# A memory-attention and gated feed-forward block: a shorter feature map, statistics on ScalarE, reciprocal rows through DRAM, later gates and a new sorting of the plan

## The chip, the cores and the metric

The kernel runs on one core of a Trainium2 chip. The core has a matrix engine (TensorE, PE in the profile, with its weight loads as PEld), a vector engine (VectorE, DVE), an engine for functions (ScalarE, ACT), a general engine (GpSimd, POOL) and a queue that issues all of this kernel's DMAs (SyncE, SP). Each engine works through its own list of instructions in a fixed order and waits on semaphores. The metric is the device time of one execution in microseconds, and the median of three runs is compared.

## What is computed

The input x has 2048 tokens of width 1024 in bfloat16. The first block is attention with a compressive memory, 32 heads of width 32 (`Dh`), over four segments of 512 tokens:

```python
x = A_x
h = x + _A_ref(_layernorm(x), wq, wk, wv, wo, beta)
h2 = h + _B_ref(_layernorm(h), w1, w3, w2)      # silu(x@w1) * (x@w3) @ w2, width 3584
...
phi = lambda t: jnp.where(t > 0, t + 1.0, jnp.exp(t))
g = _sigmoid(beta)
for s in range(4):                               # M and z start at zero
    p = _softmax(qs @ ks.T * Dh ** -0.5 + mask)  # causal, within the segment
    a_mem = (phi(qs) @ M) / (phi(qs) @ z + 1e-06)
    o = g * a_mem + (1.0 - g) * (p @ vs)
    M = M + phi(ks).T @ vs
    z = z + phi(ks).sum(0)
```

The normalisation has no weights. Only x, the weights and `beta` are read; the other input of the second block is not used.

## The kernel before

**Stages.** `run` (L1402) registers the operations: constants and the normalisation, transposition and first projections of segment 0 (`constants`, `first_half`), normalisation of the other three segments (`ln1`), then for each segment the projections of the next one (`qkv`) and two halves of attention with 16 heads each (`attention`). The output projection with the residual and the second normalisation of four token tiles of 128 (`wo_stage`) follows for segment 0 after its attention, for segment 1 inside segment 2, for segments 2 and 3 inside the feed-forward part. That part has two blocks of 1024 tokens: `ffn_up` in 14 chunks of 256 columns and `ffn_down`.

**One half of attention.** Heads are packed in groups of four, one head (`j`) to each 32 partitions. `scores` computes key-by-query scores in ten steps (`i` 0 to 9). Each step fills PSUM banks 0 to 3 (L1094), ScalarE takes the exponential of 2048 columns into tile `et[i]` (L1108), and POOL zeroes the upper triangle by `affine_select` (L1117). Steps 0 to 4 belong to the first pair of groups, steps 5 to 9 to the second. `gather` (L1122) adds the exponentials of several key chunks into `sums` on DVE (L1128), so that the denominators need fewer columns. `finish` (L1145) then issues the numerators (one matmul block for each `j`, 16 matmuls, L1180), the denominators against a tile of ones (48 matmuls, L1180, into bank 4, preceded in segments 1 to 3 by four matmuls for the memory's denominator, L1173) and the memory update phi(k) times v (L1022, into bank 7). `DEN_AT = 2` registers the denominators after the numerators of `j` 0 and 1; the planner is free to turn that round.

**Reciprocals.** The denominators are transposed on DVE (`T1`, L1211), 1e-6 is added to the memory's part, and the reciprocal is taken (`Rc`, L1222). Row 0 of `Rc` belongs to the softmax, row 1 to the memory. The softmax part is spread over the partitions by two DVE transposes of a broadcast (`spread` into `R0`, L1243), and four products `Nsb * R0` follow on POOL or DVE (L1274). The memory part in segment 1 is spread in the same way into `R1`. In segments 2 and 3 (`ROWS`), `copies` does it through DRAM: a POOL copy, a DVE transpose into `T2`, a DMA to `r_scr` and four DMAs that each read four rows for all of 32 partitions (L1263). `retrieve` is held back until step `LATE` (3) of the next half; it multiplies phi(q) with the memory (L1292), combines the result with `gcol` and `R1` on DVE (L1305), which frees PSUM banks 0 to 3, and adds it into `oT` (L1308).

**Feature map.** `phi` (L985) works on 1024 columns at a time, 12 times for keys and 12 times for queries. The exponential is taken on ScalarE into the single buffer `phe` (L712 in the profile), DVE limits it to 1 (L989), the positive part of the input is taken on POOL, ScalarE or DVE as the planner decides (L993, L994), and DVE adds the two (L998). For keys the result is transposed by a DMA (`pkn`); for queries it goes to `pq`, which the retrieve of the half before still reads.

**Normalisation.** `ln` (L867) takes the statistics by `ln_stats` on DVE (two `bn_stats`, one `bn_aggr`, L861 and L864), or by `ln_act` on ScalarE with two passes that accumulate, if the tile's number is in `ON_ACT`. Tiles 0 to 15 are those of x and 16 to 31 those of h. In the kernel before `ON_ACT` is empty; only `first_tile` uses `ln_act`, for tiles 1 and 3. The reciprocal square root is on POOL.

**Gates.** `constants` (L798) loads `beta`, takes tanh(beta/2) on ScalarE in four operations and makes `gcol` (the gate) and `ocol` (one minus the gate) on DVE (L826, L828). They are first needed by the copies of the numerators into `Nsb` (L1231, L1232).

**Order of the work.** The order on each engine is not that of registration. `Graph` collects operations with their dependences, and `schedule` simulates the five engines in advance: at each moment a free engine takes, among operations whose inputs would be there, the one with the lowest class (`cls`), and among those the lowest sequence number. The durations in this simulation are written into the kernel: `dve_ns`, `act_ns`, `pool_ns` and `mm_ns`, and for a DMA 1.9 us after its bytes at 260 bytes a nanosecond, all DMAs one after another. The resulting order is emitted as it is. Where an operation takes longer on the chip than in the plan, the engines behind it wait. Groups of operations that share a PSUM bank take it when it is free: the dense matmuls of projections and of the feed-forward part use banks 5, 6 and 7 (after the attention the others too), and have the lower priority, so that they fill the time between the steps of attention. `port=True` in an operation tells the planner that DVE and POOL hold each other up. `SHIFT` gives for each unit of work (`stage()` starts one) an offset of the sequence number and of the class.

Of the kernel before, what the change touches and what calls it, by code (L numbers as in the profile page):

```python
# [18 lines left out]
DEN_AT = 2  # L19
DIRECT = False  # L20
BOTH2 = True
ROWS = (2, 3)
ADDED = ((1, 2, 3),) * 4
ON_ACT = ()
# [3 lines left out]
    3: (-320, -1), 4: (0, 1), 5: (-481, 0), 6: (-334, -1), 7: (365, 0), 8: (-1541, -1),  # L28
    9: (99, -1), 10: (865, 1), 11: (368, -1), 13: (140, 0), 14: (6, -1), 15: (18, 0),
    16: (-1206, 0), 17: (-918, 0), 18: (-6, 1), 19: (-488, 0), 20: (-215, 1), 21: (414, 1),  # L30
    23: (-58, 0), 24: (0, 1), 25: (-7, 0), 26: (-82, -1), 28: (-682, -1), 29: (-1308, -1),
    30: (-6603, 0), 31: (429, -1), 32: (-651, 0), 33: (-3176, 0), 34: (-496, 0), 35: (-1076, 0),
    36: (-624, 0), 37: (-1589, 0), 38: (0, -1), 39: (-4, 0), 40: (-277, 0), 41: (-320, 1),
    42: (-3785, 1), 43: (-148, 0), 44: (1693, 0), 45: (72, 0), 46: (275, 0), 48: (1583, 1),
    49: (299, 0), 50: (1122, -1), 51: (-1111, 0), 52: (-3085, 0), 53: (1277, 0), 54: (1912, 1),
    55: (491, 0), 56: (52, 0), 57: (-78, 0), 58: (-1228, 0), 59: (-7, 0), 60: (-103, 0),
    61: (501, 0), 62: (-112, 1), 63: (89, 0), 64: (-177, -1), 65: (-1143, 0), 66: (228, -1),
    67: (3315, -1), 68: (484, 0), 69: (-163, 1), 70: (2537, 1), 71: (-380, 0), 72: (833, 0),
    73: (1731, 0), 75: (-2092, -1), 76: (-155, 0), 77: (839, 1), 79: (108, 0), 80: (0, 1),
    81: (338, 1), 82: (697, 1), 83: (-320, 0), 84: (285, 0), 85: (1217, -1), 86: (-2242, 0),  # L40
    87: (-180, -1), 88: (2991, 1), 90: (1277, 0), 91: (252, -1), 92: (1203, 1), 93: (2098, 0),
    94: (5, 0), 95: (1349, 0), 98: (-244, -1), 99: (-14, 0), 100: (1667, 1), 101: (-47, 0),
    102: (-85, 1), 103: (1174, 0), 106: (-1638, 1), 107: (1004, 1), 108: (-1222, 1),
    109: (-48, -1), 110: (2537, 0), 111: (-15, 1), 112: (-447, 0), 113: (1690, 1),
    114: (-550, 0), 115: (-277, 0), 116: (-328, 1), 117: (1477, -1), 118: (37, 0),
    119: (-36, 0), 120: (-1378, -1), 121: (-1111, 1), 122: (232, -1), 123: (-401, 0),
    124: (-488, 1), 125: (94, 1), 127: (66, -1), 128: (252, 0), 129: (255, -1), 130: (501, -1),
    132: (28, 0), 134: (2, 1), 135: (856, -1), 136: (95, 0), 137: (482, 0), 139: (158, 1),
    140: (-291, 0), 142: (447, 0), 143: (-390, -1), 144: (90, -1), 145: (1198, 1),
    146: (200, 0), 147: (-180, 0), 148: (-885, -1), 149: (0, 1), 150: (-1249, 0), 151: (256, 0),  # L50
    152: (-567, -1), 153: (1731, 1), 154: (206, 0), 155: (-1573, 1), 156: (278, 0),
    158: (2418, 0), 159: (-1065, 1), 160: (1955, 1), 161: (288, -1), 162: (1035, 0),
    163: (-1029, 0), 164: (-1294, 1), 166: (60, -1), 167: (-1, 0), 168: (-846, 0),
    169: (255, 0), 171: (959, 1), 172: (-62, 1), 173: (-714, 0), 174: (-77, 0), 175: (716, -1),
    176: (-158, 0), 177: (117, 0), 178: (-3360, 1), 179: (153, -1), 180: (-594, 0),
    181: (-875, 0), 182: (-1181, 1), 184: (14, 1), 185: (-1260, 1), 186: (-2791, 1),
    187: (-183, -1), 188: (0, 1), 189: (1102, -1), 191: (-526, 0), 192: (-372, 0), 193: (0, -1),
    194: (25, 1), 195: (466, 0), 196: (-1098, 1), 197: (182, 1), 198: (-410, 1), 199: (0, 1),
    200: (-350, 1), 201: (-704, 1), 202: (17, 0), 203: (-224, 0), 204: (-1609, -1),
    206: (491, 0), 207: (37, 1), 208: (-945, 0), 209: (-2625, -1), 210: (1203, 0),  # L60
    211: (-734, 1), 213: (1780, 1), 214: (618, 1), 215: (-271, 0), 219: (-57, 0), 220: (0, -1),
    221: (547, -1), 222: (1095, 1), 223: (-4674, -1), 224: (-159, 0), 225: (69, 0),
    226: (62, 0), 227: (-44, -1), 229: (1014, 1), 230: (-818, 0), 231: (610, 1), 232: (92, 1),
    233: (1, -1), 234: (-337, 1), 235: (724, 0), 237: (269, 0), 238: (-488, 0), 240: (694, 1),
    241: (1020, 0), 243: (-219, 1), 244: (-349, 1), 245: (-238, -1), 246: (-1310, -1),
    247: (1154, -1), 248: (351, -1), 250: (581, 0), 251: (-68, 0), 252: (-940, 1),
    253: (365, 0), 254: (466, -1), 255: (-4, 0), 256: (-1012, 0), 257: (1144, 0), 258: (432, 0),
    259: (88, 0), 260: (3, 1), 261: (80, 0), 262: (-4, 0), 263: (64, 1), 265: (223, -1),
    266: (-216, -1), 267: (-860, 0), 268: (-236, -1), 269: (1156, 0), 270: (-238, 1),
    271: (-107, 1), 272: (432, 1), 273: (-432, 0), 274: (-3355, 1), 275: (1256, 1),  # L70
    276: (1764, 1), 277: (-77, 0), 278: (-279, 0), 279: (-567, 0), 280: (-2286, 1),
    281: (-89, 0), 282: (-3, 0), 283: (-69, -1), 284: (-111, -1), 285: (-2, 0), 286: (-110, 1),
    287: (-370, 0), 288: (-52, 0), 289: (-1782, -1), 290: (-1781, -1), 291: (45, 0),
    293: (-846, -1), 294: (521, 0), 295: (-1210, 0), 296: (1213, 1), 297: (696, 1),
    298: (967, 0), 299: (-16, 0), 300: (-138, 0), 301: (20, 0), 302: (1085, 0), 303: (9, 0),
    304: (-1097, 1), 305: (-649, 1), 306: (-2220, 1), 307: (0, -1), 308: (-635, 0),
    309: (10, 0), 310: (596, 1), 311: (694, 0), 312: (316, 1), 314: (1928, 1), 315: (-123, 0),
    316: (-138, -1), 317: (166, 0), 318: (612, 0), 319: (416, -1), 320: (1725, -1),
    321: (857, 0), 322: (278, -1), 323: (1764, 0), 324: (-69, 0), 326: (366, 1), 327: (-79, 0),
    328: (-1240, 0), 329: (356, 0), 330: (1509, 0), 331: (-1173, 0), 332: (284, -1),  # L80
    334: (715, 0), 335: (1178, -1), 336: (0, -1), 337: (82, -1), 338: (-85, 0), 339: (-308, 0),
    340: (-186, -1), 341: (-228, 0), 342: (-1134, 1), 344: (-424, 0), 345: (221, 0),
    346: (269, 0), 347: (1885, -1), 348: (1209, 0), 349: (690, 0), 350: (50, 0), 351: (-777, 0),
    352: (2, 0), 353: (-1040, 0), 354: (-6, 0), 355: (96, 1), 356: (952, 0), 357: (274, 0),
    358: (-6, -1), 359: (142, -1), 360: (-51, 1), 361: (-4, 0), 362: (25, 0), 363: (85, 0),
    364: (313, -1), 365: (-53, -1), 366: (693, -1), 367: (-158, 1), 368: (-612, -1),
    369: (173, 0), 370: (-1556, -1), 373: (-163, 1), 375: (-1005, 0), 376: (220, 0),
    377: (-15, 0), 379: (173, -1), 380: (13, 0), 381: (577, 0), 382: (1277, 0), 384: (0, -1),
    386: (2981, 0), 387: (953, 1), 388: (3969, 0), 389: (-280, 0), 390: (-238, 0),
    391: (281, 0), 392: (27, -1), 393: (-1832, 1), 394: (1902, 1), 395: (-131, 0),  # L90
    396: (1049, 0), 399: (-17, -1), 400: (381, 0), 401: (-259, -1), 402: (597, 0),
    403: (-240, -1), 404: (-1784, -1), 405: (5, 1), 406: (-7, 0), 407: (906, 0), 408: (274, 0),
    409: (-1006, 0), 410: (-8, -1), 411: (58, 0), 412: (-27, 0), 414: (1052, -1),
    415: (-766, 0), 418: (-9, 0), 419: (-1, -1), 420: (2, 0), 421: (-7, 0), 423: (-22, 0),
    428: (-8, 0), 431: (-3, 0), 432: (40, 0), 433: (235, 0), 435: (-1134, 0), 436: (92, 0),
    437: (-751, -1), 438: (1339, -1), 439: (4, -1), 441: (977, -1), 443: (-1217, 0),
    444: (-3, 0), 446: (1178, -1), 447: (-687, -1), 448: (467, 0), 449: (-246, 0),
    450: (-18, 0), 451: (3, 0), 452: (1, 0), 453: (-4, 0), 454: (-120, 0), 457: (26, 0),
    459: (110, 0), 460: (-976, -1), 461: (99, 0), 462: (792, 0), 465: (1926, 0), 466: (347, 0),
    467: (3, 1), 468: (1, 1), 469: (-860, 1), 470: (2868, 0), 471: (267, 0), 473: (-7, 0),  # L100
    475: (-523, -1), 476: (-1557, -1), 477: (-1805, 0), 478: (-79, 0), 479: (-689, 0),
    480: (0, -1), 481: (9, 1), 482: (-6, -1), 483: (-149, 1), 484: (-481, 0), 485: (34, 0),
    486: (-27, 0), 487: (-1251, 0), 488: (-6, 0), 489: (0, -1), 490: (-1298, 1), 494: (445, 0),
    495: (185, -1), 496: (631, -1), 497: (-933, 0), 498: (45, 0), 499: (326, 0), 500: (4, 0),
# [483 lines left out]
def dve_ns(n, mode=1):  # L588
    return 150.0 + n / (0.96 * mode)
# [897 lines left out]
```

## Time and profile before

| | |
|---|---|
| timed runs | 894.58 us median of 3 (892.8 to 895.2) |
| profiled execution | 890.75 us, span 889.0 us, granted clock 1.0 |
| TensorE busy | 881.4 us (99%) |
| VectorE busy | 465.9 us (52%) |
| ScalarE busy | 298.9 us (34%) |
| GpSimd busy | 205.7 us (23%) |

TensorE counts as busy from the start of a matmul to its modelled end, and matmuls overlap, so small waits between two of them are seen better from the starts in the timeline than from the busy share. The first 420 us hold all of the attention, and there DVE is at 14 to 20 of each 22 us, ScalarE at 12 to 17 in most and POOL at 5 to 16. From 420 us on TensorE works through feed-forward matmuls only, together with the output projections of segments 2 and 3. The chain of work that ended last, in order of time, tells at each point which engine TensorE waited for.

### The profile page before, as it was taken

Reading aid. Unit: us, or ns where it says so; the run is one execution under the profiler, and the core shown is the slowest. Engines: PE = TensorE matmul, PEld = TensorE weight load, DVE = VectorE, ACT = ScalarE, POOL = GpSimd, SP = SyncE. Lnnn points to the kernel's source line nnn. Section 1 sums busy time; section 2 is a strip of 40 time slices with the busy share of each in tenths; the row PEclk is TensorE's granted clock in tenths of the full one; section 3 lists DMA queues with packets and bytes.
Section 4 is the critical chain, followed back from the end, with each engine's and each line's share of the span. In section 5 each row is a group of like instructions: output and inputs, shape, how many; then the busy total and the mean of one; then the engine's idle time right before and its main releaser. Section 6 shows DMA issues by size and latency. Waiting matters only on the chain.

```text
span 889.0 us, 13629 instructions
## 1 busy us (share of the span) xinstructions
PE 881.4 (99%) x5821; PEld 398.2 (45%) x5821; DVE 465.9 (52%) x710; ACT 298.9 (34%) x319; POOL 205.7 (23%) x239
## 2 busy tenths in 40 slices
PE   8999999999999999999999999999999999999998
PEld 5344444443444344444444444444444444444445
DVE  5796988779786879774546311212234343332111
ACT  5767776767555656521111100000112111110000
POOL 3747364656462735310100000000000000000000
DMA  7889958563652418195437310013131321301111
GB/s 237 235 170 227 236 154 172 184 144 107 170 139 71 132 58 180 51 305 143 170 90 178 100 43 24 30 48 95 48 95 48 112 72 49 94 1 29 42 36 48
DMA packets 148027, 101.55 MB, mean 114 GB/s; under 512 B 46080, under 2 KB 134144, under 8 KB 147456
## 3 DMA queue, kind: packets, MB, share of 16 engines
q1 hardware_dynamic: 147968, 100.69, 42.9%
q8 instruction: 46, 0.75, 0.4%
q14 instruction: 13, 0.11, 0.0%
HBM read 80.75 MB, written 9.44 MB: 101 GB/s over the span
## 4 chain that ended last, share of the span: by engine, by line
PE 92%; POOL 3%; DMA 2%; DVE 2%; SPq 1%; issue 0%; ACT 0%
PE ps L737 86%; PE ps L1180 3%; PE ps L1094 3%; SPq L314 1%; POOL pq L994 1%; DMA beta<-in_A_beta_dram 1%; DMA R<-r_scr 1%; POOL oT L1308 0%; POOL Nsb L1274 0%; DVE pq L998 0%; POOL et L1117 0%; DMA r_scr<-T 0%; PE ps L1022 0%; POOL pk L994 0%; DVE R L1305 0%; PE ps L1292 0%
## 5 line engine op out<-in xcount | busy, mean ns | idle before, releaser
L737 PE MATMUL ps<-hnT,w1b 128*128 128x512 bf16 x896 | 220.2, 380 | 0.0
L737 PE MATMUL ps<-hnT,w3b 128*128 128x512 bf16 x896 | 217.6, 380 | 0.8 <-DVE t L1368 0.8
L737 PE MATMUL ps<-w2b,hm 128*128 128x512 bf16 (+2 forms) x952 | 199.1, 367 | 0.0
L1365 ACT ACTIVATE sg<-ps 128x512 bf16<-128x512 f32 x112 | 66.8, 596 | 382.6 <-PE ps L737 382.6
L1368 DVE SCALAR_TENSOR_TENSOR t<-sg,ps 128x512 bf16<-128x512 bf16 x112 | 76.7, 684 | 197.4 <-ACT sg L1365 197.1
L1108 ACT ACTIVATE et<-ps 128x2048 bf16<-128x2048 f32 x80 | 150.0, 1875 | 41.4 <-PE ps L1094 40.7
L737 PEld LDWEIGHTS ps<-w2b,hm 128*128 128x128 bf16 x952 | 90.8, 98 | 103.0
L737 PEld LDWEIGHTS ps<-hnT,w3b 128*128 128x128 bf16 x896 | 86.0, 98 | 106.6 <-issue 5.1
L737 PEld LDWEIGHTS ps<-hnT,w1b 128*128 128x128 bf16 x896 | 86.3, 98 | 105.5 <-issue 6.8
L1117 POOL TENSOR_SCALAR_AFFINE_SELECT et<-et 128x512 bf16<-128x512 bf16 x96 | 90.4, 949 | 83.2 <-ACT et L1108 83.1
L1373 DVE SCALAR_TENSOR_TENSOR hm<-t,ps 128x512 bf16<-128x512 bf16 x112 | 75.9, 684 | 28.1 <-PE ps L737 25.6
L1397 DVE TENSOR_TENSOR ob<-hr,ps 128x512 bf16<-128x512 bf16 (+2 forms) x34 | 22.3, 656 | 127.9 <-PE ps L737 127.5
L737 PE MATMUL ps<-xnT,wp 128*128 128x512 bf16 (+1 forms) x352 | 61.5, 322 | 0.8 <-DMA wp<-in_A_wq_dram 0.7
L737 PE MATMUL ps<-wo,oT 128*128 128x512 bf16 x256 | 61.6, 380 | 0.2 <-POOL oT L1308 0.2
L737 PE MATMUL ps<-hnT,wp 128*128 128x512 bf16 x256 | 60.1, 380 | 0.0
L737 PEld LDWEIGHTS ps<-xnT,wp 128*128 128x128 bf16 x352 | 27.5, 98 | 26.6 <-issue 3.7
L1308 POOL TENSOR_TENSOR oT<-Nsb,R 128x512 bf16<-128x512 f32 x22 | 29.7, 1375 | 34.5 <-DVE R L1305 34.4
L737 PEld LDWEIGHTS ps<-wo,oT 128*128 128x128 bf16 x256 | 23.7, 98 | 30.3 <-issue 3.6
L737 PEld LDWEIGHTS ps<-hnT,wp 128*128 128x128 bf16 x256 | 23.1, 98 | 29.2 <-issue 4.4
L1128 DVE TENSOR_TENSOR sum<-sum,et 128x512 bf16<-128x512 bf16 (+1 forms) x48 | 35.5, 758 | 0.1
L1094 PE MATMUL ps<-qT,kT 32*128 32x128 bf16 (+3 forms) x512 | 31.7, 301 | 0.9 <-ACT kT L760 0.8
L1128 DVE TENSOR_TENSOR sum<-et,et 128x1024 bf16<-128x1024 bf16 x32 | 31.2, 975 | 1.2 <-ACT et L1108 1.2
(93 smaller groups left out, 609.9 us busy)
## 6 DMA issues: line engine op xcount, KB each, us to landing
w1b<-in_B_w_dram SPq DMA_DIRECT2D x28, 512.0 KB, 4.0
w3b<-in_B_w_dram SPq DMA_DIRECT2D x28, 512.0 KB, 4.1
wp<-in_A_wv_dram SPq DMA_DIRECT2D x8, 1024.0 KB, 6.4
wp<-in_A_wq_dram SPq DMA_DIRECT2D x7, 1024.0 KB, 6.4
wp<-in_A_wk_dram SPq DMA_DIRECT2D x7, 1024.0 KB, 5.8
w2b<-in_B_w_dram SPq DMA_DIRECT2D x7, 1024.0 KB, 9.4
xs<-in_A_x_dram SPq DMA_DIRECT2D x16, 256.0 KB, 5.9
h<-in_A_x_dram SPq DMA_DIRECT2D x16, 256.0 KB, 3.5
```

What stands on the lines that cost most here:

```text
L314: o.emit = lambda e, g: [e.dma_start(out, in_)]
L737: return [e.matmul(p[0](gr), p[1], p[2], start=p[3], stop=p[4]) for p in part]
L1094: ins.append(e.matmul(self.bank(gr, j, 512 - 128 * kc, off), k[r, g0 + g, 128 * kc:128 * kc + 128], q[r, g0 + g, 128 * kc:512], start=True ...
L1108: return [e.activation(et[:, :, :], src, AF.Exp, scale=self.scale)]
L1117: self.pool_op(lambda e, v=v, pat=pat: e.affine_select(v, v, pattern=pat, compare_op=ALU.is_ge, fill=0.0, base=0, channel_multiplier=-1), ...
L1128: self.dve_op(lambda e: e.tensor_tensor(out, x, y, op=ALU.add), dve_ns(n, 2), [x, y], [out], 2, port=True)
L1180: ins.append(e.matmul(self.ps[32 * i:32 * i + 32, b * 512 + c0:b * 512 + c0 + n], lhsT(i, kc, j), rhs(i, j), start=kc == 0 and j == first, ...
L1308: self.either(lambda e, out=out, Ns=Ns, R1=R1: e.tensor_tensor(out, Ns, R1, op=ALU.add), 512, 2, [Ns, R1], [out], 2)
L1365: self.g.op("act", act_ns(512), lambda e, gr, sg=sg: [e.activation(sg, self.bank(gr), AF.Tanh, scale=0.5)], writes=[sg], cls=0, group=gg)
L1368: e.scalar_tensor_tensor(t1, sg, 1.0, self.bank(gr), op0=ALU.add, op1=ALU.mult)], reads=[sg], writes=[t1], cls=0,
L1373: e.scalar_tensor_tensor(dst, t1, 0.5, self.bank(gr), op0=ALU.mult, op1=ALU.mult)], reads=[t1], writes=[dst], cls=0,
L1397: self.g.op("dve", dve_ns(n), lambda e, gr, hs=hs, ob=ob, n=n: [e.tensor_tensor(ob, hs, self.bank(gr, 0, n), op=ALU.add)], reads=[hs], wri ...
```

## The change

It touches seven things.

1. `phi` no longer limits the exponential and no longer takes a positive part. DVE computes max(t + 1, 1) in one `tensor_scalar` with two operations, and a DVE `tensor_tensor` takes the minimum of this and the exponential. POOL and ScalarE have no part in it but the exponential.
2. `gather` adds in another order. The second addition for both groups of a pair at once (2048 columns) becomes one for each group (1024), and each addition is registered at the step at which its inputs exist: for the first group at steps 1 and 2, for the second at steps 3 and 4. `ADDENG` holds it on DVE.
3. `DEN_AT` is 3: the denominators are registered after three of the four numerators.
4. The load of `beta` and the gate operations move out of `constants` into `gates`, called after step 1 of the first half of segment 0; the DMA depends on that step's scores.
5. `ON_ACT` names six of the tiles of h (17 and 19 to 23): their statistics are taken on ScalarE, with a buffer `junk` of its own for the unused output. `lnst` keeps 16 rows instead of 32.
6. In segments 2 and 3 (`ROWS0`) the softmax part of the reciprocals too goes through DRAM: one write for both parts, four loads into `R0w` (over `et[6]` and `et[7]`), and after the products are registered four loads into `R1`. Its two DVE transposes go.
7. All entries of `SHIFT` are new.

```diff
-DEN_AT = 2
+GATES = 1
+DEN_AT = 3
+PHI = ("dve",)
+ROWS0 = (2, 3)
+ADDENG = ("dve",)
-BOTH2 = True
-ON_ACT = ()
+ON_ACT = (17, 19, 20, 21, 22, 23)
 SHIFT = {
-    3: (-320, -1), 4: (0, 1), 5: (-481, 0), 6: (-334, -1), 7: (365, 0), 8: (-1541, -1),
+    0: (-18, 0), 3: (-173, 0), 4: (-182, 0), 5: (1074, 0), 6: (1041, 1), 7: (-959, -1),
...
-        self.lnst = buf("lnst", [128, 32, 12], F32)
+        self.lnst = buf("lnst", [128, 16, 12], F32)
+        self.junk = buf("junk", [128, 1024], BF16)
...
+        self.R0w = buf("R0w", [128, 4, 512], F32, self.g.base[self.et[6].name][1])
...
+    def gates(self):
         self.g.dma(self.beta[:, :], bass.AP(self.A_beta.tensor, self.A_beta.offset,
-                                            [[0, 128], [1, 32]]), cls=3)
+                                            [[0, 128], [1, 32]]), cls=3, deps=(self.mark,))
...
-        self.dve_op(lambda e: e.tensor_scalar(e_, e_, 1.0, None, op0=ALU.min), dve_ns(1024, 4),
-                    [e_], [e_], cls, port=True)
-        def part(e, gr):
-            if e is self.nc.scalar:
-                return [e.activation(dst, src, AF.Relu)]
-            return [e.tensor_scalar(dst, src, 0.0, None, op0=ALU.max)]
-
-        self.g.op(("pool", "act", "dve"), {"pool": pool_ns(1024), "act": act_ns(1024), "dve": dve_ns(1024, 4)},
-                  part, reads=[src], writes=[dst], cls=cls, port=True)
-        self.dve_op(lambda e: e.tensor_tensor(dst, dst, e_, op=ALU.add), dve_ns(1024, 2),
+        self.g.op(PHI, {"pool": pool_ns(1024), "dve": dve_ns(1024, 4)},
+                  lambda e, gr: [e.tensor_scalar(dst, src, 1.0, 1.0, op0=ALU.add, op1=ALU.max)],
+                  reads=[src], writes=[dst], cls=cls, port=True)
+        self.dve_op(lambda e: e.tensor_tensor(dst, dst, e_, op=ALU.min), dve_ns(1024, 2),
                     [dst, e_], [dst], cls, port=True)
...
+        if s == 0 and not g0 and i == GATES:
+            self.gates()
...
-        if 1 in added and i in (1, 4):
-            n = i // 4
-            add(S[:, :, n, :], at[g + n, 0][:, :, 256:512], at[g + n, 1][:, :, 128:384], 1024)
-        if 2 in added and i == 4:
-            both = S.rearrange("p j n q -> p j (n q)")
-            if BOTH2:
-                add(both, both, self.et[5 * pair + 2][:, :, :], 2048)
...
+        for n, step in ((0, 1), (1, 4)):
+            todo = {0: 3 * n, 1: step, 2: 2, 3: step}
+            s, done = S[:, :, n, :], None
+            for kc in sorted((0,) + added, key=lambda kc: (max(todo[kc], todo[0]), kc != 0, kc == 3)):
+                when = max(todo[kc], todo[0])
+                if when > i:
+                    break
...
+                if when == i:
+                    if kc == 3:
+                        add(s[:, :, 128:256], s[:, :, 128:256], x, 512)
+                    else:
+                        add(s, done, x, 1024)
+                done = s
...
-        def copies(tile):
+        def flat(both):
...
+        rows0 = rows and s in ROWS0
+        if rows0:
+            flat(True)
+            copies(self.R0w, 0)
         for j in range(4):
-            if j % 2 == 0:
+            if j % 2 == 0 and not rows0:
                 spread(self.R0[:, :, :], 0, j // 2)
-            Ns, R0 = self.Nsb[j][:, :], self.R0[:, j % 2, :]
+            Ns, R0 = self.Nsb[j][:, :], self.R0w[:, j, :] if rows0 else self.R0[:, j % 2, :]
...
-        last = copies(self.R1) if rows else [
+        if rows and not rows0:
+            flat(False)
+        last = copies(self.R1, 4 if rows0 else 0) if rows else [
             spread(self.R1[:, 2 * n:2 * n + 2, :], 1, n) for n in range(2)]
```

## The prediction

> **What bounds the kernel now.** I read the head of the page first, then the chain that ended last in order of time, then the timeline of the places where that chain leaves TensorE, and last the groups of the operations that the change touches.
>
> ```profile
> span 889.0 us, 13629 instructions
> PE 881.4 (99%) x5821; PEld 398.2 (45%) x5821; DVE 465.9 (52%) x710; ACT 298.9 (34%) x319; POOL 205.7 (23%) x239
> ...
> PE 92%; POOL 3%; DMA 2%; DVE 2%; SPq 1%; issue 0%; ACT 0%
> ```
>
> TensorE (PE) is busy for 99% of the span and the chain is 92% TensorE. The change adds no matmul and removes none, so it can only move three things: time in which TensorE stands still, time that it loses when it changes between kinds of matmul, and the idle start. The first two are read from the chain.
>
> ```profile
> 10.19 7.42 DMA beta<-in_A_beta_dram
> 17.64 0.21 ACT gcol L712
> ...
> 18.11 0.61 ACT kT L760
> ...
> 18.76 0.39 PE ps L1094 x4
> ...
> 51.70 2.29 PE ps L1180 x64
> 53.99 2.70 PE ps L737 x12
> 56.69 1.21 PE ps L1180 x48
> 57.90 0.97 PE ps L737 x4
> 58.87 0.59 PE ps L1022 x64
> 59.46 0.97 PE ps L737 x4
> ...
> 294.10 5.26 DMA R<-r_scr
> ...
> 299.60 0.52 PE ps L1292 x16
> ...
> 300.20 2.79 POOL pq L994
> ...
> 303.01 1.75 DVE pq L998
> ...
> 378.25 41.56 PE ps L737 x192
> ```
>
> Columns: start, length, what. First block: the gate operations stand ahead of a kT eviction in ScalarE's queue and wait for beta; the first scores wait for that eviction. Second block: numerators (x64), denominators (x48) and the memory update (x64) of one half, with dense matmuls between them. Third: the retrieve matmuls wait for the rows from DRAM, and then the feature map's POOL step holds DVE.
>
> The last line prices a dense matmul: 41.56/192 = 0.2165 us. From the starts of consecutive matmuls in the timeline I measured what each wait of TensorE adds to that pace. After the start-up there are six, 2.70 us in all: 0.84 at 18.76 (beta), 0.31 at 207.59 (oT), 0.15 and 0.06 at 259.15 and 261.28 (after a POOL pq), 0.34 at 299.60 (the rows R), 1.00 at 306.16 (after a POOL pq). From 420 us to the end there is none. Start-up (8 us to the first projection) and the last 2.6 us aren't touched.
>
> **Changing between kinds of matmul.** Twelve dense matmuls cost 12 x 0.2165 = 2.60, but the run between two other kinds takes 2.70; four cost 0.87 and take 0.97. A 512-column score group takes 0.33 where a dense matmul takes 0.22. So one interruption of the dense stream costs 0.10 + 0.11 = 0.21 us. There are some 100 of them (80 score groups, 8 halves with up to three column blocks, 6 retrieves), about 21 us.
>
> [...] the same pq addition takes 0.67 at best and 1.75 under a POOL step. [...] the trace has one table load for Exp, Tanh, Copy and Square, so the moved gates and statistics add none.
>
> **The change, part by part** (group view by form, mean ns).
>
> ```profile
> L994 POOL TENSOR_SCALAR pk<-kT 128x1024 bf16<-128x1024 bf16 x6 | 18.2, 3035 | 5.9 <-ACT kT L760 5.6 <-DVE kT L761 0.3
> L994 POOL TENSOR_SCALAR pq<-qT 128x1024 bf16<-128x1024 bf16 x4 | 11.5, 2869 | 3.1 <-PE ps L1292 2.4 <-DVE qT L761 0.7
> ```
>
> *Feature map.* Of 24 maps each loses its min on DVE (24 x 0.70 = 16.8 us) and its relu (10 on POOL, 29.7 us; 12 on ACT, 12.4; 2 on DVE, 0.8). It gains one DVE tensor_scalar with two operations; its nearest row is the relu on DVE, 0.398, so 9.6 us. The final step stays a DVE tensor_tensor (min for add). DVE -8.0, POOL -29.7, ACT -12.4 us. None of this is on TensorE. But the order is planned by written costs, and the planner's 1024-element POOL cost is 210 + 0.88 x 1024 = 1.11 us against 2.87 to 3.04 measured. TensorE's fixed order therefore arrives early: three places (207.59, 259-261, 306.16) come after such a POOL step, 0.31 + 0.21 + 1.00 = 1.52 us. Bounds: 0 recovered, 1.52 recovered; DVE's planned 0.42 and 0.68 are the measured ones (0.40, 0.68), so I take all of it, -1.5.
>
> *Gates later.* One DMA, four Tanh (0.21 each) and two DVE operations leave the start. SP has only four x loads behind beta there, needed much later. The evictions behind the Tanh go ahead, the others of that stage being done by 17.6; the whole 0.84 goes. At the new place the DMA follows the second scores (22.7 us) on SP, beside a 1 MB wq load at 22.79; wp loads land after 6.4 us, so beta may again be later than planned and hold ScalarE, with an Exp behind it, which the next scores need. Bounds 0 to 0.8 lost; an Exp slot of 3.0 us holds 1.9 of Exp, so most is absorbed: 0.2.
>
> *Sums and DEN_AT.* Per pair two additions of 1024 replace one of 2048: 32 x 0.975 - 16 x 1.348 = +9.6 us on DVE, but behind the last Exp of a pair now only one 1024 and one 512 remain (0.98 + 0.46) instead of 1024, 2048 and two 512 (3.2). The denominators are ready about 1.8 us sooner, and come after three numerators (1.7 us). In the old order they follow their numerators directly in 2 of 8 halves and are behind 4 to 12 dense matmuls in six; the memory update comes after four more dense matmuls in all its six, because the planner offers it only once the denominators are over. The fourth numerator now fills that moment. So up to 12 interruptions can close: 0 to 12 x 0.21 = 2.5 us. Bank 7 must be free for the denominators; I take 8, -1.6 or -1.7.
>
> *Statistics on ScalarE.* Six tiles: DVE -6 x (2 x 0.681 + 0.198) = -9.4; ACT + 6 x (1.057 + 0.186 + 1.150 + 0.187 + 2 x 0.194) = +17.8. With the feature map ACT is +5.4 of 889. ScalarE runs 14 to 16 of each 22 us between 110 and 220. A 1.1 us pass ahead of an Exp is planned at its true length. 0, hidden by the dense matmuls. The smaller lnst reuses rows read long before: 0.
>
> *Rows R0 over DRAM, segments 2 and 3.* Eight DVE transposes go (8 x 1.225 = 9.8 us); 16 DMAs of 256 KB are added, four in each half between the T write and the R1 loads. The round trip in the old trace is 3.07 (write) + 6.6 (first issue to last landing, 292.80 to 299.36) = 9.7 us. The planner has 3.0 + 5.9 at best, so the products Nsb x R0 on DVE or POOL may stand for 0.7 us, with PSUM evictions behind them on DVE, and R1 comes behind four more loads (1 us each by the planner's rate). The 0.34 at 299.6 stays; bounds 0 to 1.5 us more per half, I take 0.1 in each: +0.4. In sum DVE has -8.0 + 9.6 - 9.4 - 9.8 = -17.6 us, worth nothing by itself.
>
> *Shifts.* New sorting of about all units: costs nothing in itself, but every wait above is newly dealt. Inside the numbers' uncertainty.
>
> **Sum.** -0.84 - 1.5 - 1.7 + 0.2 + 0.4 = -3.4 us, span 889.0 to 885.6. The profiled execution took 890.75; the three timed ones have a median of 894.58 (892.8 to 895.2), so I lay the difference on that: 894.58 - 3.4 = 891.2. From the same terms the most is -0.84 - 1.86 - 2.5 = -5.2, some 889.4, and a start-up or score groups better placed might add 1.
>
> **Rivals.** (A, 0.52) as above, own range 888.5 to 891.9. (B, 0.28) The waits are only moved: the blocks stay broken up because bank 7 is held, beta is late at its new place (0.8 lost again), the new order has as many small waits as the old, 1.5 to 2.7 us. Then -0.8 to +1: 893.8 to 895.6. For it: no order here is free of them. Against: the POOL step with the worst planned cost is gone. A measurement can't tell 0.3% (2.7 us, the spread of the three times) from no change. (C, 0.17) Slower: the products with R0 stand on DVE until the four row loads land, and dense evictions stand behind them; three PSUM banks of 1.73 us each cover some 2 us. Each us beyond that is a us of TensorE. To end at +0.3% it has to eat 3.4 + 2.7 = 6.1 us, 1.5 in each of four halves, so DVE held for 3.5 us per half; R loads issued in busy stretches took up to 7.9 us to land where 5.3 is the quiet figure, so the late loads reach this only when planned early. It would give 898 to 901. (D, 0.03) More than A: 887 to 888.5, by score groups that close up with the column blocks.
>
> **How the numbers follow.** The time is A's, 891.2. A ends at the limit of 0.3% (891.9), so faster is A with D, less the part of A that measures short: 0.53; same 0.29; slower 0.18. The range: below 888.3 only D lies, above 896.5 only C with the end of B; 888.3 to 896.5 leaves out 0.2.
>
> **What would show it.** Right: no beta DMA before the first scores and these at about 17.9 us; no POOL feature-map row, one DVE row of x24 near 0.4 us; in the chain numerators, denominators and the memory update (L1022) of a half with no dense run between; sum of TensorE's waits after start-up under 1.5 us; TensorE still 99%. Wrong: TensorE waits on a DVE eviction behind Nsb x R0, on DMA R0w, or on an Exp behind gcol; or the dense runs of four between column blocks are all still there.

## The result, and the profile after

The changed kernel takes 888.17 us (median of 4 runs, 887.12 to 888.86), the kernel before beside it 894.50 (892.8 to 895.2): ratio 0.9931, 95% interval 0.9914 to 0.9948. A second measurement of both, described below, gave 0.9949 (0.9937 to 0.9962). By these two ratios the change is worth 4.5 to 6.2 us, 0.5% to 0.7%.

Head of the page and the chain's shares, changed kernel:

```profile
span 886.3 us, 13649 instructions
PE 873.0 (99%) x5732; PEld 400.5 (45%) x5821; DVE 449.2 (51%) x699; ACT 302.5 (34%) x345; POOL 178.4 (20%) x226
...
PE 94%; DMA 2%; DVE 2%; issue 1%; POOL 0%; ACT 0%; SPq 0%; ACTq 0%; POOLq 0%; DVEq 0%
```

TensorE bounds it as before (the trace lacks 89 matmul records, so the weight loads, x5821, are the better count: none came or went). POOL has gone from the chain, where it had 3%. DVE lost 16.7 us, where the prediction had 17.6. Now the same places of the chain in order of time (start, length, what):

```profile
16.59 0.81 PE ps L747 x3
17.40 0.33 PE ps L1101 x4
...
126.02 4.42 PE ps L747 x20
130.44 1.74 PE ps L1194 x48
132.19 0.22 PE ps L1187 x4
132.40 1.64 PE ps L1194 x64
134.04 0.52 PE ps L1029 x64
...
295.02 8.92 DMA R0w<-r_scr
...
304.11 1.28 POOL Nsb L1296
...
305.41 1.26 DVE oT L1332
...
309.47 1.04 PE ps L747 x4
```

The first scores (L1101) start at 17.40, straight behind dense matmuls, with no gate operation and no DMA in between. In the second block the column work of a half, which the old chain showed with dense runs of 4 and 12 matmuls in between, is one stretch: numerators and denominators (L1194), the memory's denominator (L1187), the memory update (L1029). All eight halves look like that; counted over the whole trace, the dense stream enters a column block 8 times instead of 20. By the starts of the matmuls, and with 0.2165 us taken off for each dense one, this half takes 4.23 us where it took 4.62 (two interruptions closed); over the eight halves it is 2.3 us less. The third block is new: the rows `R0w` come through DRAM, land 8.92 us after the last of their loads was issued, and behind them stand the products, the combination into `oT` and an eviction that TensorE waits for, 0.55 us by the pace of the matmuls.

The feature map in the groups (busy, mean ns of one | idle before):

```profile
L1003 DVE TENSOR_SCALAR pq<-qT 128x1024 bf16<-128x1024 bf16 x12 | 7.2, 604 | 0.0
L1003 DVE TENSOR_SCALAR pk<-kT 128x1024 bf16<-128x1024 bf16 x12 | 7.1, 602 | 0.1
```

In 10 of the 24 maps this DVE step of 0.60 us replaces a POOL step of 2.9 to 3.0 us, in 12 a ScalarE step of 1.05 and in 2 a DVE step of 0.40; in all 24 the DVE limit of 0.70 us goes as well.

### The profile page after: what moved, and what is told of

Its sections match the earlier page's. It is cut to its first block, busy times and chain, and to the rows that moved or that the text cites. A ratio compares the mean times of both kernels' runs of the same rounds, so it can differ in the third digit from the quotient of the medians.

```text
span 886.3 us, 13649 instructions
## 1 busy us (share of the span) xinstructions
PE 873.0 (99%) x5732; PEld 400.5 (45%) x5821; DVE 449.2 (51%) x699; ACT 302.5 (34%) x345; POOL 178.4 (20%) x226
## 4 chain that ended last, share of the span: by engine, by line
PE 94%; DMA 2%; DVE 2%; issue 1%; POOL 0%; ACT 0%; SPq 0%; ACTq 0%; POOLq 0%; DVEq 0%
PE ps L747 88%; PE ps L1194 3%; PE ps L1101 3%; DMA R0w<-r_scr 1%; DMA r_scr<-T 1%; DVE oT L1332 0%; SPq L1281 0%; DMA xs<-in_A_x_dram 0%; PE ps L1029 0%; DVE lnst L874 0%; ACT et L1115 0%; PE ps L1316 0%; POOL et L1124 0%; DVE hm L1397 0%; PE ps L1187 0%
## 5 line engine op out<-in xcount | busy, mean ns | idle before, releaser
L1124 POOL TENSOR_SCALAR_AFFINE_SELECT et<-et 128x512 bf16<-128x512 bf16 (+1 forms) x96 | 93.1, 976 | 133.0 <-ACT et L1115 132.7
L747 PE MATMUL ps<-xnT,wp 128*128 128x512 bf16 (+1 forms) x345 | 59.6, 320 | 1.3 <-issue 0.8
L1138 DVE TENSOR_TENSOR sum<-sum,et 128x512 bf16<-128x512 bf16 (+1 forms) x64 | 43.6, 684 | 11.6 <-POOL et L1124 6.1
L1101 PE MATMUL ps<-qT,kT 32*128 32x128 bf16 (+3 forms) x512 | 31.7, 301 | 0.0
L747 PE MATMUL ps<-wp,xnT 128*128 128x512 bf16 x123 | 30.2, 379 | 0.4 <-issue 0.2
L747 PE MATMUL ps<-wp,hnT 128*128 128x512 bf16 x123 | 29.6, 380 | 0.5 <-issue 0.3
```

Of the source, the lines that this page charges most:

```text
L747: return [e.matmul(p[0](gr), p[1], p[2], start=p[3], stop=p[4]) for p in part]
L1101: ins.append(e.matmul(self.bank(gr, j, 512 - 128 * kc, off), k[r, g0 + g, 128 * kc:128 * kc + 128], q[r, g0 + g, 128 * kc:512], start=True ...
L1124: self.pool_op(lambda e, v=v, pat=pat: e.affine_select(v, v, pattern=pat, compare_op=ALU.is_ge, fill=0.0, base=0, channel_multiplier=-1), ...
L1138: lambda e, gr: [e.tensor_tensor(out, x, y, op=ALU.add)], reads=[x, y],
```

## Experiments

All runs were made beside the kernel before, and a ratio is to that, unless said otherwise. My theory is the prediction's: TensorE's places count (the gates at the start, the waits behind POOL's feature map, the broken column blocks), and the loads of DVE, POOL and ScalarE don't. The main rival is that waits only move. Where an experiment moves an operation, the order that the planner made stays as it was apart from it; the short lines with - and + then sketch that order and are not code.

**The two kernels again** (b_same, a_same): no edit.

> The kernel before, unchanged. The profiled execution of it took 890.75 us and the timed ones 892.8 to 895.2, while after shows no such gap (887.99 against 887.1 to 888.9). Theory: the timed executions of before hold some 3 us of waiting that the profiled one escaped, at a place that depends on how DMAs land (beta in front of the first kT eviction, or the R rows before a retrieve). Then this profile, if it comes out above 892, shows a wait of TensorE of 2 to 4 us more at one of those places. Rival: an execution of before with a profile is always near 890, and the gap belongs to the measurement; then the profile reads 889 to 891 again and the timed runs 893 to 895.

> After, unchanged, for a second profile and beside the other kernels. In the profiles so far the matmuls from the last retrieve to the end waited for late weight loads for 1.0 us (before), 2.9 (the kernel before once more), 1.8 and 1.1 (its two variants), and 0.7 in after. Theory: a good part of the 5 to 6 us between the timed runs is that after waits less for weight loads; then it reads 888.2 again, 5.5 us under before, and again under 1 us of such waiting. Rival: the first runs of after were lucky; then 889.5 to 890.5, and the loads cost it 1.5 to 2.5 us too.

The old kernel against itself gave 1.0004 (0.9994 to 1.0014), its executions lying between 891.3 and 896.9 (57 runs, median 893.66). The changed kernel gave 888.42, ratio 0.9949, executions between 887.5 and 889.6. So the old kernel scatters over 5.6 us in 57 executions; the nine of the new one lie within 2.5, but so few would show a smaller spread in any case. The profile shown with the prediction took 890.75 us, less than any of those 57. An execution of 893.28, near the median, has in its chain:

```profile
448.68 5.42 DMA w3b<-in_B_w_dram
...
454.15 0.60 PE ps L737 x2
454.81 3.40 PE ps L737 x15
```

TensorE waits here for a weight load of the feed-forward part, 1.35 us by the pace of the matmuls, and not at beta or the rows, where I had expected the missing time: these cost 0.80 and 0.37 us, as in the first profile. In the eight profiled executions with the old kernel's order (the kernel before, b_same and the six b_ experiments below) this wait appears in four, with 0.5 to 1.3 us of idle time; in six of the changed order (the changed kernel and its experiments) in none. Late weight loads elsewhere occur in both: a_late waits 0.57 us at 612 us, a_best three times before 130 us.

**Gates alone** (b_gates): in the kernel before, only the beta load, the four Tanh and the two DVE operations are moved.

```
-order: beta load, 4 x Tanh, 2 x gcol/ocol at the start
+order: beta load at 24.0 us, Tanh at 36.0, gcol/ocol at 37.0 of the plan
```

> Before, with only the load of beta, the four Tanh and the two DVE gate operations put later (load at about 24 us of the plan, Tanh at 36); every other instruction keeps its place in its engine's order. Theory of the prediction: the first scores come at 17.9 us instead of 18.76 and the time falls by 0.8 us, to about 893.7; if the late landing of beta is also what lengthens the timed executions, by 2 to 4 us, to 891 to 892. Rival: other evictions of the start end no sooner, or the next wait takes it over: 0, 894.5.

891.84, ratio 0.9979 (0.9970 to 0.9988): 1.9 us (1.1 to 2.7), the largest median of the single parts tried, though its interval overlaps that of the next one. The first scores now follow dense matmuls directly:

```profile
19.12 0.81 PE ps L750 x3
19.93 0.33 PE ps L1107 x4
```

They come at 19.9 us and not at the 17.9 that was expected, because this execution (893.96 us, one of the slowest of its 21) has TensorE at half clock for 3.4 us from 8.8 us on, which costs 1.7 us, in the start-up and before any gate operation. In b_all, which has the gates moved too and no such stretch, they come at 18.3 us. So the gain of this part rests on the times. The traces show what it removes: in the six profiles that keep the old place of the gates, the wait behind beta is 0.62 to 1.62 us.

**The positive part on POOL shortened** (b_relu): the kernel before, POOL takes max(x, 0) over 128 of 1024 columns (except at a buffer's first use), so the map is incomplete.

```
+            if e is self.nc.gpsimd and not first:
+                return [e.tensor_scalar(dst[:, 0:1, 0:128], src[:, 0:1, 0:128], 0.0, None, op0=ALU.max)]
```

> Before, with the positive part of the feature map on POOL computed for 128 of its 1024 columns, except at the first use of each buffer (left out: seven eighths of those POOL steps; the order of all engines is that of before). A POOL step falls from 2.8 to about 0.5 us. Theory of the prediction: the waits at 207.6, 259 to 261 and 306.2 us go, -1.5 us, to about 893.0. Rival: POOL's length only changed which operation is named last, and DVE or the R rows make TensorE wait there all the same: 0 to -0.4, 894.2 or more.

891.78, ratio 0.9983 (0.9972 to 0.9994): 1.5 us, what the prediction had for the feature map. Its chain at the place where the old one waited 1.00 us:

```profile
299.93 0.44 PE ps L1296 x16
300.37 1.83 PE ps L737 x8
302.26 4.26 PE ps L737 x19
306.52 0.33 PE ps L1098 x8
```

The retrieve (L1296) still waits for `R` (0.38 us); after it TensorE runs through to the next scores.

**Column blocks, both ways** (b_mem, a_open). In b_mem the memory update of six halves follows the denominators directly, which closes 6 of the 12 interruptions. In a_open 14 dense operations of the changed kernel are put back between the column blocks.

```
b_mem   -num  dense  den  dense(4)  mem      a_open  -num den num mem   dense ...
        +num  dense  den  mem  dense(4)              +num dense den dense num dense mem ...
```

> Before, with the memory update put directly behind the denominators in all six halves that have one: the dense operation of four matmuls between the two goes behind it. Six interruptions of the dense stream less, nothing else moved on any engine. Theory: 6 x 0.21 = -1.3 us, 892.4. Rival: an interruption costs nothing of itself [...]: 0, 893.7.

> After, with the column blocks broken up again: in each of the eight halves one dense operation of four matmuls is put between numerators and denominators (or before the memory update), and in the six halves with a memory update a second one before it; 14 interruptions more on TensorE, no other engine's order changed. Theory: 14 x 0.21 = +2.9 us, 891.1. Rival: the time was won by the waits and not by the blocks, or the broken blocks only fill waits that stand there anyway: +0 to +1, 888 to 889.

b_mem: 892.36, ratio 0.9990 (0.9980 to 1.0000), -0.9 us where 6 x 0.21 = 1.3 was expected. The interval reaches from -1.8 to 0, so the times alone don't exclude the rival, that an interruption costs nothing. The trace speaks against it: by the starts of the matmuls each of the six halves is 0.17 to 0.18 us shorter, 1.05 us together. Its chain in one half:

```profile
96.76 1.21 PE ps L1193 x48
97.97 0.52 PE ps L1035 x64
```

a_open: 894.53, ratio 1.0011 (1.0004 to 1.0018), the whole gain and more gone, 6.0 us between its span and the changed kernel's where 2.9 was expected. This run is not a clean dose. Of the 14 interruptions five are made up for elsewhere, because scores now follow a block directly; the net nine are some 2 us at most. The rest are waits that the edit itself made:

```profile
PE ps L1114 <- ACT Nsb L1258: 3.7, 3, 1.4
```

(Waiting instruction, what it waited for, us in total, times, longest.) Scores that had a dense run ahead of them now stand directly behind the numerators and wait for the `Nsb` evictions. Which part of the 6 us the interruptions hold can be said from the trace only roughly.

**Late loads in the second feed-forward block** (b_late, a_late): in each kernel the units from number 523 lose their shifts, so that fewer weight loads there are issued just ahead of their use.

```
-            late, cls = SHIFT.get(o.unit, (0, 0))
+            late, cls = SHIFT.get(o.unit, (0, 0)) if o.unit < 523 else (0, 0)
```

> Before, without the shifts of the second feed-forward block (units from 523 on); the order of all engines is that of before up to 545 us of the plan. The number of 512 KB weight loads that the plan issues only 4.1 us ahead of their first matmul falls from 11 to 4 and the planned span stays the same. Theory: such loads land after 4.1 us in the median and up to 8.9, so executions lose 1 to 2 us on them at random: 892.3 to 893.0 and a narrower spread than 891.3 to 896.9. Rival: late loads are hidden by the matmuls queued ahead or happen before 545 us: no change, 893.7.

> After, without the shifts of the second feed-forward block; same order up to 551 us of the plan. Loads with 4.1 us of lead fall from 13 to 3. Theory: after still loses some 0.5 us there, so 887.7, a little under after. Rival: after loses nothing there: 888.2 as after, or the plain order costs matmul pace: above 889.

b_late 1.0004 (0.9996 to 1.0012), a_late 0.9963 (0.9949 to 0.9977) against the kernel before, no better than a_same. The expected gain is not there. b_late's 13 executions do lie closer together (892.0 to 894.2) than the 25 beside them (891.6 to 895.0); whether that is the loads is open; the ones that the trace shows late lie before 460 us and were not tried by themselves.

**Three parts at once** (b_all): gates, short POOL step and closed memory update of b_gates, b_relu and b_mem in one kernel.

> The kernel before with three parts at once: the gate operations later, the positive part of the feature map on POOL taken over 128 of 1024 columns (apart from the first use of each buffer; the output is then not the reference's), and the memory update directly behind the denominators in six halves. Alone they gave -1.8, -1.5 to -1.9 and -0.9 us. Theory 1 (the parts add up, and with 6 of the 12 closed interruptions they carry most of the change): -4.0 to -4.8 us against the kernel before, ratio 0.9946 to 0.9955, and in the profile no wait of TensorE over 0.5 us between the first score and 320 us. Rival (the parts share one slack, so that a wait taken away in one place comes back in the next): -2.0 to -2.8 us, ratio near 0.997.

890.11, ratio 0.9958 (0.9946 to 0.9970), -3.8 us. The parts' ratios multiply to 0.9952; the rival's 0.997 is the edge of the interval. Adding up is the better account, and a small shared part is not excluded. In its trace one wait over 0.5 us is left before 320 us, which I had not expected: 0.73 us for the rows at 298 us.

**DVE's load** (b_dve): the bn_stats of tiles 16 to 31 read 64 of 512 columns.

```
+            w = b[:, 0:64] if k >= 16 else b
-            self.dve_op(lambda e, a=a, b=b: e.bn_stats(a, b), 650.0, [b], [a], cls, deps=deps)
+            self.dve_op(lambda e, a=a, w=w: e.bn_stats(a, w), 650.0, [b], [a], cls, deps=deps)
```

> The kernel before with the statistics of the sixteen tiles of h (16 to 31) taken over 64 of 512 columns in each bn_stats (the variance and mean are then of a part of the row), the order of all queues kept. DVE loses some 32 x 0.5 = 16 us of work, about as much as the change takes from it (465.9 to 449.2). Theory 1 (DVE's load is off the path; the gain lies in places): 0, ratio 0.9995 to 1.0005. Rival (part of the gain is DVE's lower load, evictions come sooner everywhere): -1 to -2.5 us, ratio 0.997 to 0.999.

```profile
PE 874.6 (98%) x5723; PEld 398.4 (45%) x5821; DVE 450.4 (51%) x710; ACT 299.2 (34%) x319; POOL 206.7 (23%) x239
```

DVE has fallen to 450.4 us, nearly the changed kernel's 449.2, and the time is 893.90, ratio 1.0005 (0.9993 to 1.0017). Fifteen microseconds of DVE, taken from the normalisation of h, buy nothing; the rival's 1 us or more lies outside the interval. DVE's work between the steps of attention was not tried by itself.

**The rows' place in the DMA queue** (a_r0first): in the changed kernel the planner had put the `R0w` loads behind the `R` loads in three of four late halves; here they go ahead of them.

```
-SP: r_scr<-T, R x4, R0w x4
+SP: r_scr<-T, R0w x4, R x4
```

> The changed kernel with the four R0w loads of the second, third and fourth late half issued ahead of the four R loads instead of behind them (in the first they are ahead already). Nothing else is moved. Theory 1 (the two sets of rows share one queue, and what stands second pays): the retrieve at 299 us, which waits for R and stood still for 0.92 us, waits 1.5 to 3 us longer, and the wait of 0.55 us at 311 us, behind the products with R0w, goes; in sum +0.5 to +2.0 us, ratio to the changed kernel 1.0005 to 1.0022, to the kernel before 0.994 to 0.9965. Rival (the rows land together, whatever their order, or the waits there are not for the rows): no change, within 0.4 us, and both waits stay.

902.0 (899.9 to 905.7), ratio 1.0092 (1.0072 to 1.0112): about 13 us over a_same, more than six times the top of what I had expected. TensorE's timeline at the three retrieves of the profiled execution (start, busy, what, in brackets the idle time before):

```profile
304.84 0.66 PE L1329 MATMUL ps<-pq,Mbf 32*32 32x512 bf16 x16 [6.15 <-DMA R<-r_scr]
...
352.78 0.66 PE L1329 MATMUL ps<-pq,Mbf 32*32 32x512 bf16 x16 [2.32 <-issue]
...
411.62 0.66 PE L1329 MATMUL ps<-pq,Mbf 32*32 32x512 bf16 x16 [2.95 <-DMA R<-r_scr]
```

and stretches around the first of them and behind all three (stretch, its length, busy time with count of PE, PEld, DVE, ACT, POOL, then PEclk, DMA share, GB/s):

```profile
299.80:304.80 5.00, 0.00 (x0) 0.00 (x0) 0.00 (x0) 0.00 (x0) 0.00 (x0) 0.67 0.68 141
304.80:308.40 3.60, 3.37 (x23) 1.25 (x25) 2.69 (x4) 0.60 (x1) 2.77 (x3) 0.51 0.00 0
308.40:312.00 3.60, 3.60 (x17) 1.53 (x16) 3.08 (x6) 0.60 (x1) 3.60 (x4) 1.00 0.86 214
...
352.70:356.30 3.60, 3.41 (x23) 1.29 (x25) 2.65 (x5) 0.00 (x0) 3.08 (x3) 0.53 0.26 64
...
411.60:415.20 3.60, 3.58 (x24) 1.21 (x25) 2.71 (x5) 0.00 (x0) 1.27 (x1) 0.50 0.48 124
415.20:420.00 4.80, 4.80 (x18) 1.93 (x17) 2.62 (x5) 0.60 (x1) 2.87 (x2) 0.76 0.44 139
```

The direction was mine: what stands second pays. The size wasn't, for two reasons. The row loads that stand second land late: 8.70, 8.39 and 10.40 us after the last of the `R` loads is issued, against 5.85, 5.59 and 7.31 in the changed kernel, where `R` stands first. The writes ahead of them take nearly the same in both (5.8, 2.0 and 11.1 us against 5.4, 2.0 and 10.1), so it is the order. Two of these loads in the chain:

```profile
295.90 8.70 DMA R<-r_scr
...
401.09 10.40 DMA R<-r_scr
```

`R` is what TensorE itself waits for, while `R0w`, standing second in the changed kernel and landing after 8.92 us, is read by POOL and DVE and cost TensorE 0.55. And each of the three waits, 11.4 us together against 0.85 in the changed kernel, is followed by a stretch at half clock: by the trace's clock records 3.5, 3.3 and 5.9 us after TensorE starts again (the third reaches into the last line above, with 0.76). Half of each is lost, 6.4 us in all. Both make 17 us; the span of this execution is 16.7 over the changed kernel's. It is one of the slower of six; all six have a granted clock under 1 (0.991 to 0.996, the changed kernel 1.0), so the median's 13 us hold both parts too.

**An attempt at a better version** (a_best): in the changed kernel one dense operation of four matmuls ahead of the numerators at 175 us, and one ahead of the retrieve at 299 us.

```
-PE at 175 us: numerators, denominators, memory update, dense(4)   at 299 us: retrieve, dense(4)
+PE at 175 us: dense(4), numerators, denominators, memory update   at 299 us: dense(4), retrieve
```

> The changed kernel with two dense operations of four matmuls put earlier, everything else in its place: one ahead of the numerators at 175 us, which waited 0.30 us for their exponentials, and one ahead of the retrieve at 299 us, which waited 0.92 us for the rows. Theory 1 (these are plain waits that a filler of 0.87 us covers): -0.6 to -1.2 us against the changed kernel, some 887.3, ratio to the kernel before 0.9925 to 0.994. Rival (the time turns up at the next wait, such as the evictions of the banks that the filler takes, or the scores behind it): 0 to -0.3 us.

889.48 (887.8 to 892.1), ratio 0.9954 (0.9941 to 0.9967). Both waits that it aimed at are gone (0.30 and 0.92 us by the matmuls' pace), but the 0.55 us at 309 has become 0.49 at 305 and 0.78 at 311, behind the same kind of eviction. Only half a microsecond is left of the 1.2, and the execution profiled has other waits ahead of that:

```profile
PE ps L760 <- DMA wp<-in_A_wq_dram: 2.1, 3, 0.9
```

So no version here is better than the changed kernel.

## Why the prediction was right, and where its terms were off

Faster was predicted, at 891.2, and faster it is; the mechanism of case A holds in the main. The size was short: -3.4 predicted, -4.5 to -6.2 measured. The 888.17 lies 0.1 us below the range's end of 888.3, the second measurement's 888.42 as much above it, both in the stretch of case D. D's own reason, score groups that close up, did not come about: the dense stream enters the scores 80 times before and after. By its terms:

- **Gates, -0.84 + 0.2.** Mis-sized. The term was one wait in one execution. Alone the move gives -1.9 (interval -1.1 to -2.7). In the traces the first scores come at 18.6 to 19.6 us in the kernel before and its experiments (without b_gates and b_all), at 17.3 to 18.0 in the changed kernel, with eight 128-column matmuls (0.45 us) fewer ahead of them: about 1.0. What beta costs depends on when it lands: in six profiles 0.62, 0.79, 0.80, 0.83, 1.54 and 1.62 us. The 0.84 was an ordinary value and not an average; what b_gates gains beyond 1.0 is not explained. The new wait of +0.2 isn't there: the beta load is issued at 20.38 us, and TensorE waits for no gate operation.
- **Feature map, -1.5.** Right: b_relu gives -1.5 (-0.5 to -2.5) and the three waits are gone in its trace. The DVE step takes 0.60 us in the mean and not the 0.40 of the relu that I took as its nearest row, with no effect that a run shows.
- **Column blocks, -1.6 or -1.7.** Mis-sized: all 12 interruptions closed, where I took 8. In the trace the closed blocks are 2.3 us shorter, 0.19 for each, close to the prediction's upper bound of 2.5. "Bank 7 must be free for the denominators" was the reason for 8, and no half shows it. b_mem, with six of them, gave 0.9 in its times and 1.05 in its trace. Whether the new `DEN_AT`, the earlier sums or the new shifts closed them was not tried.
- **Statistics on ScalarE, 0, and DVE's 17.6 us, "worth nothing by itself".** For DVE shown by b_dve, as far as the normalisation of h goes. The statistics' move to ScalarE was not tried by itself; ScalarE rose from 298.9 to 302.5 us, with one table load of 1.28 us in both traces.
- **Rows, +0.4, "the 0.34 at 299.6 stays".** The wait stays and varies: 0.92 us at 299.05 in one execution of the changed kernel, none over 0.1 in a_same, with 0.55 and 0.30 us behind the products at 309. Against the old 0.34 that is +1.1 in one execution and nothing in the other. The +0.4 lies between them by luck, for a reason that I had not seen: the planner put the loads of `R`, which I feared to find "behind four more loads", ahead of them in three halves of four. In the other order the same loads cost 13 us more. That was the slower rival C's transfer, but at the retrieve and not, as C had it, at DVE's products.
- **What the sum lacked.** The difference was laid on the median, but its waits were read from the execution of 890.75 us, which had fewer of them than most. What an ordinary execution loses besides, late weight loads and late beta, the new order seems to lose less often: 0.5 to 1.3 us at 454 us in four of eight old profiles and in none of six new. That this comes from the new order is not shown: the profiles are few, b_late and a_late did not reach that place, and no run tries a shift there.
- **Rival B, waits only moved.** Partly so. Between the first scores and the last retrieve TensorE waits 1.1 to 2.3 us in three profiles of the changed order (the changed kernel, a_same, a_late), against 1.9 to 3.0 in four of the old (the kernel before, b_same, b_late, b_dve): the removed 1.5 us came back in part as row and eviction waits. The blocks and the start carry the rest.

Gates 1.0 to 1.9, blocks 2.3, waits in the middle about 0.4 net (the means of these profiles), late weights about 0.5 (the mean over the old ones): 4.2 to 5.1 us, at the lower end of the 4.5 to 6.2 measured. Shown by runs of their own are the gates, the shorter POOL step and, with b_all, that they add to the closed memory update. The sums with `DEN_AT`, the statistics, the rows through DRAM as a whole and the shifts were not tried alone.

The prediction said what would prove it right: no beta load before the first scores and these at about 17.9 us (17.3 to 18.0), no POOL row in the feature map, one DVE row of x24 near 0.4 us (two rows of x12, 0.60), closed blocks, under 1.5 us of waits (1.1 to 2.3: met in one of three profiles). Of its signs of being wrong one shows, in small: the eviction behind the products with `R0w`, 0.30 to 0.55 us.

## To carry to other kernels

Where one engine is busy for 99% of the span, cost a change by the places where that engine stands still or changes between kinds of work (0.19 us for each closed interruption here), and not by the work that other engines lose: 15 us of DVE in a normalisation bought nothing, a few operations out of ScalarE's queue at the start 1.9 us. Read these places in more than one execution, since the wait for one DMA was a spread here and not a number (beta: 0.62 to 1.62 us in six profiles). If two sets of transfers share a queue, look up which of them the bounding engine itself waits for: their order alone was worth 13 us here, in part because TensorE ran at half clock for 3.3 to 5.9 us after each of three waits.

## What the runs showed of the hardware beyond that

- TensorE stood at half clock after idle times of 6.15, 2.32 and 2.95 us in a_r0first, for another 3.5, 3.3 and 5.9 us once it worked again, which cost 1.7, 1.7 and 3.0 us. After 0.85 us in the changed kernel, 1.48 in b_late and 1.55 in b_relu it kept full clock; after 1.51 us in the start-up of b_gates it did not, for 3.4 us. So each of the three waits of over 2 us in a_r0first cost 1.7 to 3.0 us on top. The 1.51 and 1.55 us ended in opposite ways: these runs show no idle time that divides the two.
- A POOL tensor_scalar over 1024 bf16 columns took 2.9 to 3.0 us in the mean (2.77 to 3.43) in the kernel before, the DVE step with two operations that replaced it 0.60. Of the 24 of these DVE steps in the changed kernel's trace, the 15 that began with no POOL step under way (in one it ended 0.01 us later) took 0.37 to 0.43 us; the nine that began with 0.28 us or more of a POOL step still to run took 0.56 to 1.32.
- Of POOL's 32 `affine_select` steps over 1024 columns in the kernel before, 17 took 1.10 or 1.11 us and seven 1.61 or 1.62; each of the seven began within 0.05 us of the start of a DVE addition (L1128).
- Four row loads of 256 KB that stand second in the queue landed 8.4 to 10.4 us after the last of them was issued in a_r0first (8.46 to 10.09 in the changed kernel's three late halves with `R0w` second). The write of 256 KB ahead of them took anything from 2.0 to 11.1 us in the same program (2.01 and 11.07 in a_r0first).
